# Moving the evacuation of the turned attention rows from VectorE to ScalarE, with the softmax reciprocals multiplied on GpSimd

## The chip, the core and the metric

The kernel runs on one core of a Trainium2 chip. Five engines work side by side, each through its own list of instructions in order: PE (TensorE, the matrix products), DVE (VectorE), ACT (ScalarE), POOL (GpSimd) and SP (SyncE, which here only issues DMA transfers). An instruction starts when its engine has come to it and the semaphores that it waits for have been raised. Products are written to PSUM, a small memory of eight banks that PE, DVE and ACT reach; POOL and the DMA transfers work on SBUF. The metric is the time of one execution in microseconds (us), the median of several runs.

## The reference, cut to what matters

Windowed attention with a distance bias, then a layer that sends each token to one of eight experts, then a dense two-layer network. The change lies in the first part and touches the rows that feed the second.

```python
scores = scale * np.matmul(q, k.transpose(0, 1, 3, 2))
scores = np.where(mask, scores + bias[None], -1000000000.0)      # mask: 0 <= i - j < 128
scores = scores - np.max(scores, axis=-1, keepdims=True)
attn = np.exp(scores)
attn = attn / (np.sum(attn, axis=-1, keepdims=True) + 1e-09)
attn_out = np.matmul(attn, v)                                    # 4 batches, 8 heads, 576 rows, 64 wide
x = attn_out.transpose(0, 2, 1, 3).reshape(B * S, H * D)         # 2304 rows of 512
...
logits = x @ w_gate + modality_bias[modality_id]
e_idx = np.argmax(logits, axis=1)
```

## The kernel before, in words

**Stages.** Attention fills the first 150 us. Then come the expert products, the chunks left over, and the dense network, which is by far the longest part; only attention is touched by the change. The program order of every engine is the order in which the code is written: nothing is reordered by a scheduler.

**Units.** Attention works on 40 units (b, t, hh): a batch b, a stretch t of 128 query rows (the fifth, t = 4, has 64), and a half hh of the eight heads. Two units make a row tile, and a group g of 128 output rows is one row tile, or the two short ones of two batches. There are 18 groups, of which 16 have t < 4. Line numbers are those of the kernel before, with L for line.

**A step.** The main loop takes step k and, in this order, issues: `smax` of unit k (DVE: pick the right columns, L289 or L284, then add the bias and take the row maximum, L294 or L296), the first half of `sexp` of unit k (ACT: the exponentials, L315 or L317), `sc` of unit k + 1 (PE: the scores into the banks called s and t), `tr` and `ev` of unit k - 2 (PE turns the exponentials, L337; ACT copies them out of the bank v, L344, L347 or L350; POOL masks the copy, L354 and L355), the second half of `sexp`, a first call of `background()`, `pv` of unit k - 3 (PE: the product with v, L374 or L381, into the bank W0, called x in the rows), and a second call of `background()`. For t = 4 two more ACT multiplications (L329) normalise the exponentials.

**The group's tail, `post`.** When both halves of a row tile are in W0, `post` is put on a list that `background()` works through, one piece at each call. Piece 1 (the second call in step k): ACT copies W0 to SBUF (L394). Piece 2 (the first call in step k + 1): PE multiplies that copy by `turned` (L403), which turns the rows back and also gives the gate's logits. The result has 4 blocks of 144 columns; three go to the bank called m, the fourth goes to the second half of W0, which is free at that time. DVE adds 1e-9 to the row sums and takes reciprocals (L405, L406). Piece 3 (the second call in step k + 1): DVE takes the result out of both banks and multiplies it by the reciprocals on the way (L418; for t = 4 it only copies, L416): 384 and 128 columns of rows (`row<-m`, `row<-x`) and 48 and 16 columns of logits (`ls<-m`, `ls<-x`). It then sums the logits (L419), and SP writes the rows to HBM (L420). The products `pv` of the next row tile's first half come between pieces 2 and 3 in the code, and write the first half of W0.

**Around it.** Every third group or so starts `route` (L450 to L508), a chain of small DVE operations with a few products, one piece at each call of `background()`. In the last third of attention the first expert slot is prepared between the units: gathers on POOL (L716), casts of weights and of gathered rows on ACT (L669, L730), the second half of a split on POOL (L672) or DVE (L734), and the first expert products on PE (L743).

Of the kernel before, what the change touches and what calls it, by code (L numbers as in the profile page):

```python
# [13 lines left out]
ALU = mybir.AluOpType  # L14
# [4 lines left out]
B, H, S, D = 4, 8, 576, 64  # L19
NTOK, DM = B * S, H * D  # L20
E, FF = 8, 1024
# [18 lines left out]
def row_of(g):  # L40
    return 128 * g + (SLOT if g >= CHECK else 0)
# [12 lines left out]
def attention_moe_kernel(ctx, tc, qh, kh, v, mid, wg, mb, w1, w2, win, wout, out):  # L54
    nc = tc.nc
    dve, act, pe, pool = nc.vector, nc.scalar, nc.tensor, nc.gpsimd
# [20 lines left out]
    def row(dt=F32):  # L77
        return take(("row", dt), 6, lambda: rowp.tile([128, DM], dt, tag="row", name="row"))

    def bank(tag, shape=(128, 512)):  # L80
        n = 1 if tag in "xm" else 2
        return take((tag, tuple(shape)), n, lambda: psum.tile(list(shape), F32, tag=tag, name=tag, bufs=n))
# [4 lines left out]
    xs = [[dram.tile([128, 2, 2, HT], F32, name=f"xs{j}_{i}") for i in range(7)] for j in range(NB)]  # L87
# [269 lines left out]
    def group(u):  # L357
        b, t, _ = u
        return 9 * (b // 2) + (8 if t == 4 else 4 * (b % 2) + t)
# [4 lines left out]
    def pv(u):  # L364
        b, t, hh = u
        o = st.pop(u)
        kb = [4] if t == 4 else [t - 1, t] if t else [t]
        for i in range(2):
            hp = 2 * hh + i
            if t < 4:  # L370
                for n, k_ in enumerate(kb):
                    for j in range(2):
                        h = 2 * hp + j
                        pe.matmul(W0[64 * j:64 * j + 64, hp, :], vS[b][:, k_, 64 * h:64 * h + 64], o[:, i, k_ - t + 1, j, :], start=n == 0, stop=n == len(kb) - 1, skip_group_check=True)  # L374
            else:
                c = slice(64 * (b % 2), 64 * (b % 2) + 64)
                for n in range(2):
                    r = 64 if n else 128
                    for j in range(2):
                        h = 2 * hp + j  # L380
                        pe.matmul(W0[64 * j:64 * j + 64, hp, c], vS[b][:r, 3 + n, 64 * h:64 * h + 64], o[:r, i, n, 0, 64 * j:64 * j + 64], start=n == 0, stop=n == 1, skip_group_check=True)  # L381
        if hh:
            todo.append(post(u))
# [3 lines left out]
    def post(u):  # L387
        b, t, _ = u
        g = group(u)
        if t < 4 or b % 2 == 0:  # L390
            xus[g] = row().rearrange("p (a b) -> p a b", a=4)
        xu = xus[g]
        c = slice(64 * (b % 2), 64 * (b % 2) + 64) if t == 4 else slice(0, 128)
        act.copy(xu[:, :, c], W0[:, :, c])  # L394
        if t == 4 and b % 2 == 0:
            return
        del xus[g]
        yield

        C = 128 + 2 * E  # L400
        xp = bank("m")[:, :3 * C].rearrange("p (a c) -> p a c", a=3), W0[:, 2:4, :].rearrange("p a b -> p (a b)")[:, None, :C]
        for i in range(4):
            pe.matmul(xp[i // 3][:, i % 3, :], xu[:, i, :], turned[:, i, :], start=True, stop=True)  # L403
        if t < 4:
            dve.tensor_scalar(rinv[b, t], rinv[b, t], 1e-9, None, op0=ALU.add)  # L405
            dve.reciprocal(rinv[b, t], rinv[b, t])  # L406
        yield
        xs = row()
        ls = sm.tile([128, H, E], F32, tag="ls", name="ls", bufs=2)
        r = rinv.pop((b, t)) if t < 4 else None  # L410
        for p, h0, n in ((xp[0], 0, 6), (xp[1], 6, 2)):
            hs = slice(h0, h0 + n)
            for o, w, d in ((xs.rearrange("p (h d) -> p h d", h=H)[:, hs, :], p[:, :, :128], D), (ls[:, hs, :], p[:, :, 128:], E)):
                o, w = o.rearrange("p (a j) d -> p a j d", j=2), w.rearrange("p a (j d) -> p a j d", j=2)
                if t == 4:
                    dve.tensor_copy(o, w)  # L416
                else:
                    dve.tensor_tensor(o, w, r[:, hs].rearrange("p (a j) -> p a j", j=2)[:, :, :, None].to_broadcast([128, n // 2, 2, d]), op=ALU.mult)  # L418
        dve.tensor_reduce(l_all[:, g, :], ls.rearrange("p h e -> p e h"), axis=AX.X, op=ALU.add)  # L419
        nc.sync.dma_start(out=xd[row_of(g):row_of(g) + 128, :], in_=xs)  # L420
        if g in gends:
            ready.append(route(g + 1 - gends[g], gends[g]))
# [362 lines left out]
    def expert_src(e, j):  # L785
        src = w1 if j < 4 else w2
        return src[bass.ds(e, 1), j % 4].rearrange("o p f -> (o p) f")
# [183 lines left out]
    n = len(units)  # L971
# [129 lines left out]
    for s in range(NSLOT):  # L1101
        n, nn = ({NSLOT - 1: SHORT, NSLOT - 2: MIDDLE}.get(i, SLOT) for i in (s, s + 1))
# [26 lines left out]
        if s == 2:  # L1129
            p = bank("v", (128, E))  # L1130
# [6 lines left out]
        for i in range((n + 127) // 128):  # L1137
# [3 lines left out]
            c = slice(128 * i, min(n, 128 * i + 128))  # L1141
# [24 lines left out]
    p = ps = None  # L1166
    held.append({})

    def chunk(src):
        r, h, l = (take(("w", dt), n, lambda: wpools["right"].tile([128, 1024], dt, tag="w", name="w")) for dt, n in ((F32, 2), (F32R, 4), (F32R, 4)))  # L1170
        nc.sync.dma_start(out=r, in_=src)
        act.copy(h, r)
        dve.tensor_tensor(l, r, h.bitcast(F32), op=ALU.subtract)
        return h, l

    le, lo = (loop_int[:, i].rearrange("p a b -> p (a b)") for i in range(2))
    with tc.For_i(4 * (NSLOT - 1), total, 1) as ci:
        e = nc.sync.value_load(le[0:1, bass.ds(ci, 1)], min_val=0, max_val=E - 1)
        o = pool.value_load(lo[0:1, bass.ds(ci, 1)], min_val=0, max_val=E * NCH - 1)
# [4 lines left out]
        for g in range(2):  # L1184
            r, p = row(), bank("v", (128, 4, 128))
# [12 lines left out]
        for f in range(8):  # L1198
            if f % 2 == 0:
                w = chunk(expert_src(e, 4 + f // 2))  # L1200
# [13 lines left out]
    ps, c = bank("t"), slice(128 * i, 128 * i + 128)  # L1214
# [203 lines left out]
    for n, (k, h) in enumerate(((0, 0), (0, 1), (1, 1), (1, 0))):  # L1418
        for c in range(2):
            p = bank("xmssvvxm"[2 * n + c])[:, :HT]  # L1420
# [102 lines left out]
```

## Time and profile before

| what | value |
|---|---|
| median of 3 runs | 758.87 us (757.5 to 758.89) |
| the profiled execution, its own time | 757.94 us |
| span of that execution, first to last instruction | 756.1 us |
| PE busy | 725.4 us (96%) |
| DVE busy | 499.8 us (66%) |
| ACT busy | 344.4 us (46%) |
| POOL busy | 302.9 us (40%) |

The profiled execution lies inside the range of the runs. The shares are averages over the whole program. What the change is worth is decided in the first 150 us, so the rows further down come from that stretch.

### The profile page before, as it was taken

What the parts mean: (1) busy time and instruction counts of PE and PEld (TensorE: products, weight loads), DVE (VectorE), ACT (ScalarE), POOL (GpSimd) and SP (SyncE); (2) the same over time, 40 slices, a digit from 0 to 9 for tenths busy, and PEclk for the clock granted to TensorE, in tenths of its full rate; (3) what the DMA queues carried; (4) which work ended last, traced back from release to release, by engine and by line L of the source; (5) the groups of instructions that cost most, each with busy time, mean ns of one, the idle gap of its engine ahead of it and who ended that gap; (6) DMA issues with size and microseconds to landing.
All of it is one profiled execution on the core that took longest, in us unless ns stands there. A gap on an engine that the chain in (4) does not pass through costs nothing.

```text
span 756.1 us, 13418 instructions
## 1 busy us (share of the span) xinstructions
PE 725.4 (96%) x4567; PEld 627.3 (83%) x4567; DVE 499.8 (66%) x1288; ACT 344.4 (46%) x839; POOL 302.9 (40%) x328
## 2 busy tenths in 40 slices
PE   7899889999999999998989999999999999999997
PEld 6777757777788889887878898989989889899896
DVE  7788877779976967776464664466754768442542
ACT  6676658424534545454555565423324234231230
POOL 4322345303454434536162464425534246240431
PEclk9999999999999999999999999999999999999999
DMA  8558450139488685960679671879719796295832
GB/s 268 187 178 279 136 199 32 58 126 360 153 323 273 231 288 181 380 236 16 236 251 367 258 320 57 341 291 394 280 72 360 281 410 242 83 360 202 329 112 84
DMA packets 71110, 174.57 MB, mean 231 GB/s; under 512 B 10032, under 2 KB 18480, under 8 KB 71040
## 3 DMA queue, kind: packets, MB, share of 16 engines
q1 hardware_dynamic: 68048, 163.93, 59.7%
q0 software_dynamic: 2992, 9.77, 3.3%
q8 instruction: 37, 0.61, 0.3%
q14 instruction: 33, 0.27, 0.1%
HBM read 117.76 MB, written 55.90 MB: 230 GB/s over the span
## 4 chain that ended last, share of the span: by engine, by line
PE 48%; DMA 3%; DVE 1%; ACT 0%; issue 0%; ACTq 0%; SPq 0%
PE v L743 17%; PE s L743 12%; PE t L743 12%; PE x L743 3%; PE m L743 3%; DMA w<-yd 2%; DMA yd<-row,idx 1%; DVE cr L1314 1%; DVE cr L1339 0%; DVE xq L1258 0%; PE s L1355 0%; ACT hd L1306 0%; PE s L1423 0%; DVE row L1375 0%; ACT xq L1254 0%
## 5 line engine op out<-in xcount | busy, mean ns | idle before, releaser
L1307 POOL TENSOR_TENSOR hd<-cr,hd 128x384 fp32r<-128x384 f32 x96 | 113.1, 1213 | 140.9 <-ACT hd L1306 140.9
L743 PE MATMUL v<-w,hd 128*128 128x512 f32 x576 | 137.1, 390 | 0.4 <-ACT w L1358 0.4
L743 PEld LDWEIGHTS v<-w,hd 128*128 128x128 f32 x576 | 107.8, 188 | 22.6 <-ACT w L1358 0.7
L743 PE MATMUL s<-xq,w 128*128 128x384 f32 x576 | 108.1, 335 | 0.7 <-DVE cr L1339 0.7
L743 PEld LDWEIGHTS s<-xq,w 128*128 128x128 f32 x576 | 100.9, 188 | 2.1 <-issue 1.0
L743 PE MATMUL t<-w,h 128*128 128x512 f32 (+1 forms) x408 | 98.8, 395 | 2.1 <-DVE w L1213 2.1
L694 POOL TENSOR_TENSOR row<-row 128x512 int32<-128x512 int32 x32 | 45.5, 1421 | 129.7 <-DVE row L693 86.3
L743 PEld LDWEIGHTS t<-w,h 128*128 128x128 f32 (+1 forms) x408 | 73.4, 183 | 19.7 <-issue 2.6
L1306 ACT CAST hd<-cr 128x384 fp32r<-128x384 f32 x96 | 49.3, 514 | 66.4 <-DVE cr L1314 63.4
L743 PE MATMUL t<-w,hd 128*128 128x512 f32 x288 | 69.2, 389 | 0.0
L743 PE MATMUL s<-w 128*128 128x512 f32 (+2 forms) x292 | 66.2, 378 | 1.1 <-DVE h L768 1.1
L1375 DVE SCALAR_TENSOR_TENSOR row<-v,gate,row 128x512 f32<-128x512 f32 x36 | 27.0, 750 | 56.6 <-PE v L743 54.4
L315 ACT ACTIVATE e<-x,m 128x128 f32<-128x128 f32 x128 | 50.4, 398 | 30.0 <-DVE m L294 30.0
L743 PEld LDWEIGHTS t<-w,hd 128*128 128x128 f32 x288 | 54.1, 188 | 11.2
L672 DVE TENSOR_TENSOR w<-w 128x1024 fp32r<-128x1024 f32 x37 | 51.1, 1387 | 17.6 <-ACT w L669 15.5
L743 PEld LDWEIGHTS s<-w 128*128 128x128 f32 x292 | 53.2, 188 | 9.5 <-DVE h L768 2.0
L1336 ACT COPY cr<-s 128x384 f32<-128x384 f32 x48 | 23.0, 481 | 73.7 <-PE s L743 73.5
L1314 DVE SCALAR_TENSOR_TENSOR cr<-cr 128x384 f32<-128x384 f32 x72 | 52.5, 729 | 2.5
L354 POOL TENSOR_SCALAR_AFFINE_SELECT pt<-pt 128x512 f32<-128x512 f32 (+1 forms) x32 | 18.7, 586 | 75.0 <-ACT pt L350 58.7
L669 ACT CAST w<-w 128x1024 fp32r<-128x1024 f32 (+1 forms) x43 | 41.9, 990 | 2.0 <-DMA w<-w 2.0
L1339 DVE TENSOR_TENSOR cr<-t,cr 128x384 f32<-128x384 f32 x24 | 13.3, 554 | 44.1 <-PE t L743 44.1
L686 ACT ACTIVATE row<-w 128x512 f32<-128x512 f32 x32 | 21.3, 672 | 29.2 <-POOL row L694 25.6
(323 smaller groups left out, 1434.7 us busy)
## 6 DMA issues: line engine op xcount, KB each, us to landing
xq<-xs SPq DMA_DIRECT2D x42, 768.0 KB
w<-w SPq DMA_DIRECT2D x40, 512.0 KB, 5.4
xs<-xq SPq DMA_DIRECT2D x21, 768.0 KB, 3.4
ya<-row SPq DMA_DIRECT2D x54, 256.0 KB, 2.1
row<-ya SPq DMA_DIRECT2D x54, 256.0 KB, 8.8
w<-win SPq DMA_DIRECT2D x16, 512.0 KB, 7.2
wc<-row SPq DMA_DIRECT2D x32, 256.0 KB, 3.4
w<-wout SPq DMA_DIRECT2D x16, 512.0 KB, 5.2
```

The source lines that it names most:

```text
L315: act.activation(e[:, i, j, :], x[:, i, j, :], AF.Exp, bias=m[:, i, j:j + 1], scale=-1.0, accum_out=rinv[b, t][:, h:h + 1])
L354: pool.affine_select(out=diag, in_=prev[:diag.shape[0]], pattern=[[0, 2], [0, 2], [1, n]], channel_multiplier=-1, compare_op=ALU.is_ge, **kw)
L669: act.copy(h[:, c], r[:, c])
L672: (eng or dve).tensor_tensor(l[:, c], r[:, c], h[:, c].bitcast(F32), op=ALU.subtract)
L686: act.mul(f, hi.bitcast(F32), 2.0 ** -112)
L694: pool.tensor_tensor(a, a, r, op=ALU.add)
L743: pe.matmul(ps, l, r, start=first and i == 0, stop=last and i == n - 1, **kw)
L1306: act.copy(gh, c)
L1307: pool.tensor_tensor(gl, c, gh.bitcast(F32), op=ALU.subtract)
L1314: dve.scalar_tensor_tensor(c, c, 0.0, c, op0=ALU.max, op1=ALU.mult)
L1336: act.copy(c, ps[q])
L1375: dve.scalar_tensor_tensor(o, ps, gate, o, op0=ALU.mult, op1=ALU.add)
```

## The change

The multiplication by the reciprocals is taken off the way out of PSUM for the rows. ACT copies the 384 and 128 columns of rows out of the two banks as they are (the new L413). DVE still takes the 48 and 16 columns of logits, multiplied. For t < 4, POOL then multiplies the whole row tile, 128 x 512 in SBUF, by the reciprocals in place (the new L421), and the write to HBM follows that.

```diff
         for p, h0, n in ((xp[0], 0, 6), (xp[1], 6, 2)):
             hs = slice(h0, h0 + n)
-            for o, w, d in ((xs.rearrange("p (h d) -> p h d", h=H)[:, hs, :], p[:, :, :128], D), (ls[:, hs, :], p[:, :, 128:], E)):
-                o, w = o.rearrange("p (a j) d -> p a j d", j=2), w.rearrange("p a (j d) -> p a j d", j=2)
-                if t == 4:
-                    dve.tensor_copy(o, w)
-                else:
-                    dve.tensor_tensor(o, w, r[:, hs].rearrange("p (a j) -> p a j", j=2)[:, :, :, None].to_broadcast([128, n // 2, 2, d]), op=ALU.mult)
+            act.copy(xs.rearrange("p (a c) -> p a c", a=4)[:, h0 // 2:(h0 + n) // 2, :], p[:, :, :128])
+            o, w = ls[:, hs, :].rearrange("p (a j) d -> p a j d", j=2), p[:, :, 128:].rearrange("p a (j d) -> p a j d", j=2)
+            if t == 4:
+                dve.tensor_copy(o, w)
+            else:
+                dve.tensor_tensor(o, w, r[:, hs].rearrange("p (a j) -> p a j", j=2)[:, :, :, None].to_broadcast([128, n // 2, 2, E]), op=ALU.mult)
+        if t < 4:
+            o = xs.rearrange("p (h d) -> p h d", h=H)
+            pool.tensor_tensor(o, o, r[:, :, None].to_broadcast([128, H, D]), op=ALU.mult)
         dve.tensor_reduce(l_all[:, g, :], ls.rearrange("p h e -> p e h"), axis=AX.X, op=ALU.add)
         nc.sync.dma_start(out=xd[row_of(g):row_of(g) + 128, :], in_=xs)
```

In the lists of the engines, PE and SP keep their order. On DVE the second group's tail reads as follows; `m` and `x` are the two banks, `ri` the reciprocals, and the bracket at a row's end names the engines whose semaphores it waits for (Activation is ACT).

```order
 L405 TENSOR_SCALAR ri<-ri 128x8
 L406 RECIPROCAL ri<-ri 128x8 [waits DVE_49]
-L418 TENSOR_TENSOR row<-m,ri 128x384 [waits DVE_49,PE_49]
-L418 TENSOR_TENSOR ls<-m,ri 128x48
-L418 TENSOR_TENSOR row<-x,ri 128x128 [waits PE_49,Activation_49]
-L418 TENSOR_TENSOR ls<-x,ri 128x16
-L419 TENSOR_REDUCE l_all<-ls 128x8 [waits DVE_49]
+L418 TENSOR_TENSOR ls<-m,ri 128x48 [waits DVE_49,Activation_49]
+L418 TENSOR_TENSOR ls<-x,ri 128x16 [waits Activation_49]
+L422 TENSOR_REDUCE l_all<-ls 128x8 [waits DVE_49]
```

The two multiplications of rows are gone, and each of the two that are left now carries a wait for ACT where it stood behind a wait for PE.

On ACT the copies come after the second half of the exponentials. Towards the end of attention other work stands ahead of them as well; this is the piece of the changed kernel's list around group 14's evacuation, with casts of weights (L672 in its numbering) and of gathered rows (L733).

```order
L315 ACTIVATE e,ri<-x,m 128x128 [waits DVE_49] x2
L672 CAST w<-w 128x512 [waits DMAHW1_49]
L672 CAST w<-w 128x512
L733 CAST w<-v 128x2x128 [waits PE_49]
L733 CAST w<-v 128x2x128
L413 COPY row<-m 128x384 [waits DMAHW5_49]
L413 COPY row<-x 128x128
L317 ACTIVATE e,rt<-x,m 128x128 [waits DVE_49,Activation_49]
```

The two rows of L413 are new there; in the kernel before, L317 followed the casts.

On POOL one multiplication per group stands behind the masks of the step. This is a piece of the changed kernel's list, in the middle of attention.

```order
L355 AFFINE_SELECT pt<-pt 128x2x256 [waits Pool_49]
L421 TENSOR_TENSOR row<-row,ri 128x512 [waits DVE_49,Activation_49]
L354 AFFINE_SELECT pt<-pt 128x2x256 [waits Activation_49]
L355 AFFINE_SELECT pt<-pt 128x2x256 [waits Pool_49]
L354 AFFINE_SELECT pt<-pt 128x2x256 [waits Activation_49]
```

Sixteen such rows of L421 are new on POOL, and nothing is taken from it.

## Rows read from the trace of the kernel before

**Rows 1.** Attention, 16 to 150 us: busy PE, PEld, DVE, ACT, POOL; clock, DMA.

```profile
16.00:150.00 134.00, 119.48 (x1462) 95.18 (x1455) 106.00 (x582) 88.10 (x342) 50.03 (x77) 0.99 0.47 157
```

**Rows 2.** Waits of PE, 15 to 155 us (us in total, times, longest).

```profile
PE m L403 <- ACT row L394: 3.9, 8, 0.9
...
PE v L469 <- ACT pt L350: 1.2, 1, 1.2
...
PE v L469 <- DVE t_acc L508: 1.1, 1, 1.1
```

**Rows 3.** Waits of ACT, 15 to 155 us.

```profile
ACT e L315 <- DVE m L294: 26.0, 14, 3.8
```

**Rows 4.** Waits of DVE, 15 to 155 us.

```profile
DVE row L418 <- PE x L374: 5.3, 9, 0.7
...
DVE row L418 <- PE x L381: 2.1, 3, 0.7
```

**Rows 5.** The page's costliest groups: an ACT copy of 384 columns out of PSUM.

```profile
L1336 ACT COPY cr<-s 128x384 f32<-128x384 f32 x48 | 23.0, 481 | 73.7 <-PE s L743 73.5
```

**Rows 6.** ACT's groups by shape, 0 to 160 us: a copy of 256 columns.

```profile
L347 ACT COPY pt<-v 128x256 f32<-128x256 f32 x8 | 2.9, 360 | 2.5 <-PE v L504 2.5
```

**Rows 7.** Timeline of DVE and ACT about group 10's evacuation (start, duration, idle before).

```profile
90.13 0.56 DVE L418 TENSOR_TENSOR row<-m,ri 128x384 f32<-128x384 f32 x1 [0.42 <-PE m L403]
...
90.58 0.40 ACT L315 ACTIVATE e<-x,m 128x128 f32<-128x128 f32 x1
90.60 0.20 DVE L418 TENSOR_TENSOR ls<-m,ri 128x48 f32<-128x48 f32 x1
91.48 0.29 DVE L418 TENSOR_TENSOR row<-x,ri 128x128 f32<-128x128 f32 x1 [0.68 <-PE x L374]
91.69 0.17 DVE L418 TENSOR_TENSOR ls<-x,ri 128x16 f32<-128x16 f32 x1
91.88 0.27 DVE L419 TENSOR_REDUCE l_all<-ls 128x8 f32<-128x64 f32 x1
...
92.78 0.40 ACT L317 ACTIVATE e<-x,m 128x128 f32<-128x128 f32 x1 [1.71 <-DVE m L296]
```

**Rows 8.** Timeline of ACT and DVE about group 8's evacuation.

```profile
77.20 0.39 ACT L315 ACTIVATE e<-x,m 128x128 f32<-128x128 f32 x1
77.75 0.27 DVE L419 TENSOR_REDUCE l_all<-ls 128x8 f32<-128x64 f32 x1
```

**Rows 9.** Timeline of ACT and DVE about group 14's evacuation.

```profile
129.17 0.65 ACT L730 CAST w<-v 128x256 fp32r<-128x256 f32 x2
129.53 0.28 DVE L419 TENSOR_REDUCE l_all<-ls 128x8 f32<-128x64 f32 x1
...
130.43 0.40 ACT L317 ACTIVATE e<-x,m 128x128 f32<-128x128 f32 x1 [0.61 <-DVE m L296]
```

**Rows 10.** Timeline of DVE, ACT and PE about group 15's evacuation.

```profile
136.35 0.27 DVE L419 TENSOR_REDUCE l_all<-ls 128x8 f32<-128x64 f32 x1
136.45 0.65 ACT L730 CAST w<-v 128x256 fp32r<-128x256 f32 x2 [1.11 <-PE v L724]
...
139.53 1.00 PE L403 MATMUL m<-turned,row 128*128 128x144 f32 x6 [0.75 <-ACT row L394]
```

**Rows 11.** Timeline of PE, ACT and DVE about group 9's evacuation.

```profile
83.11 1.09 PE L374 MATMUL x<-pt,vS 128*64 128x128 f32 x16
83.16 0.39 ACT L315 ACTIVATE e<-x,m 128x128 f32<-128x128 f32 x1
...
85.20 0.27 DVE L419 TENSOR_REDUCE l_all<-ls 128x8 f32<-128x64 f32 x1
```

**Rows 12.** Timeline of DVE and POOL: three comparisons with and without POOL's multiplications beside them.

```profile
138.38 2.78 DVE L493 TENSOR_SCALAR row<-iota,row 128x128 fp32r<-128x128 f32 x3
138.55 2.53 POOL L672 TENSOR_TENSOR w<-w 128x512 fp32r<-128x512 f32 x2 [0.21 <-ACT w L669]
...
153.39 0.85 DVE L493 TENSOR_SCALAR row<-iota,row 128x128 fp32r<-128x128 f32 x3
```

## The prediction

> **What bounds the kernel now.** The change touches attention only, so I read that stretch and not the whole span. Over its 134 us the four busy times are 119 us for PE, 106 for DVE, 88 for ACT and 50 for POOL [rows 1]. PE is the fullest, and it has 14.5 us in which it does nothing. Only those can be won, and any new wait of PE adds to them. So the next view is what PE waits for. The waits that bear on the change are for ACT's copy L394 of the attention product (3.9 us), for ACT's copy L350 (1.2), and for DVE's small sum L508 (1.1) [rows 2]. ACT itself waits 26.0 us for DVE's row maxima, in 14 waits [rows 3]. So ACT is late because DVE is late, and PE because ACT is late. The order in a group's tail makes the loop: PE's L403, then DVE's evacuation L418 and the sum L419, then the row maxima of the next unit, then ACT's exponentials, then L394, then PE's next L403.
>
> One more view shows what holds DVE inside the evacuation. Before its second half, the 128 columns in the bank W0, it waits for PE's products L374 or L381 in 9 + 3 = 12 of the 18 groups [rows 4], although these write other columns of that bank. In group 10 it could have gone on at about 90.8 and starts at 91.48, when PE has left the bank [rows 7].
>
> **What is removed.** DVE no longer moves the 384 and 128 columns. An instruction's worth on DVE is the distance to the next start: 90.13 to 90.60 is 0.47 us, and 91.48 to 91.69 is 0.21 [rows 7]. The first of these lies in front of the wait for PE in the 12 groups that have one, so there the gain is 0.21, and it is 0.68 in the other six.
>
> **What takes its place.** The two small multiplications that stay on DVE now wait for ACT's two copies. So DVE's restart, by which I mean the start of the sum L419 after which the next row maxima follow, no longer depends on DVE's own arrival but on when ACT comes to its copies, and ACT comes to them after its four exponentials of the step and whatever else is listed ahead. I price this as follows.
>
> - ACT's copy of 384 columns takes 0.48 us [rows 5]; two casts of 256 columns take 0.65 together where a copy of that size takes 0.36, so that the next instruction starts 0.07 before the end [rows 6, 9]. That gives 0.41 from start to start.
> - No row has 128 columns. The bounds are nothing and the 0.36 of 256 columns [rows 6]. By the 0.12 us that 128 columns make between 256 and 384 [rows 5, 6] it is 0.24, an estimate that I take.
> - From DVE's second small multiplication to the sum it is 0.19 [rows 7]. The handover from ACT to DVE is not in the rows shown; nothing and 0.10 bound it, and I take 0.04.
>
> So the restart comes at the later of (ACT free + 0.41) and (PE out of W0), plus 0.24 + 0.04 + 0.19 = 0.47.
>
> **Group by group.** In group 10 ACT's last exponential starts at 90.58 and takes 0.40, so ACT is free at 90.98 and through the first copy at 91.39. PE is out of W0 at 91.48, which decides. The restart is 91.95 against 91.88 [rows 7], 0.07 later. Ten of the twelve groups that wait for PE look like this one: nothing is gained there, although DVE does less. About seven of them have a wait of PE behind them: +0.5 in all.
>
> In group 8 ACT is free at 77.59, and the restart goes from 77.75 to 78.47 [rows 8]: +0.7, and PE's wait for L508 [rows 2], which follows the row maxima, takes all of it. Group 4 is the same with +0.5.
>
> In group 14 two casts of weights and two of gathered rows stand ahead of the copies. ACT is free of them at 129.17 + 0.58 = 129.75, the restart is 130.63 against 129.53, and ACT's L317, which had waited only 0.61 us for DVE [rows 9], slips by that 1.1. PE's wait of 1.2 us for L350 [rows 2] is the one that follows: +1.1.
>
> In group 15 the copies stand behind a cast that waits for PE until 136.45. The restart goes from 136.35 to 137.91 [rows 10], and ACT itself is delayed by its own two copies, 0.65. What arrives at PE's wait for L394 at 139.53 lies between that 0.65 and the 1.56 of the restart; I take the middle, +1.1.
>
> In group 9 it is the other way. ACT was idle from 83.55 and PE out of W0 at 84.2, long before DVE arrived, so the copies are done early: restart at 84.3 + 0.47 = 84.8 instead of 85.20 [rows 11], or -0.4. Groups 6, 16 and 17 are of this kind and read in the same way: -0.3, -0.4 and -0.5.
>
> The sum is 0.5 + 0.7 + 0.5 + 1.1 + 1.1 - 0.4 - 0.3 - 0.4 - 0.5 = **+2.3 us**.
>
> **What is hidden.** POOL gets 16 multiplications of 128 x 512. Two such take 2.53 us [rows 12], so one takes 1.27, and POOL has 84 us free in the stretch [rows 1]. In group 10 it could start at 91.72; the next mask needs ACT's copy, which follows the exponential that begins at 92.78 [rows 7] and so ends after 93.5. That cover is the wait of ACT for DVE; without it each multiplication would delay a mask by up to 1.27. The write of the rows to HBM goes out about 1.3 us later. Behind it in SP's list stand loads for row tiles far ahead, and the gathers of these rows follow groups later; if a load of weights at the end were short of time it would cost that 1.3 once.
>
> **A rule beside it.** DVE's wait for PE in group 10 is for the bank, not for the columns [rows 7]. The Trainium skill, in "PSUM — Partial Sum Buffer", section "PSUM bank collisions raise a hardware error", says that no two of PE, ACT and DVE may access one bank in the same partitions at a time, reads by ACT and DVE included, and that the compiler orders such accesses one behind the other. By that rule an evacuation split between ACT and DVE is done in turns, and the sum is the one above; without it the two would read side by side and the time would be that of the first rival. The trace agrees where PE and DVE meet, with the 0.68 us of group 10; no group of before has ACT and DVE meet in this way.
>
> **Rivals.**
>
> *DVE's relief decides (faster).* Place: the restart. Price: 12 x 0.21 + 6 x 0.68 = 6.6 us less of DVE [rows 4, 7]. By the same share of about two thirds of the groups that have a wait of PE behind them some 4 us reach PE: 754 us. It decides where ACT is free 0.41 us before PE leaves the bank and before DVE arrives. For it: group 9 [rows 11], and the 26 us in which ACT is idle [rows 3]. Against it: groups 8, 14 and 15, where DVE is ahead of ACT [rows 8 to 10]. Chance 0.20.
>
> *The delays are absorbed (no change).* ACT's added work is 18 x 0.65 = 11.7 us and fits into its 26 us of waiting [rows 3]. If the late copies of groups 8, 14 and 15 fall into slack of PE that I took for none, gains and losses cancel: 757.9 to 759 us. Chance 0.18.
>
> *POOL holds up DVE (much slower).* DVE's three comparisons take 2.78 us beside two multiplications of POOL and 0.85 alone [rows 12], so one POOL multiplication can cost DVE about 1 us. If DVE has such an operation within 1.27 us of the restart in five of the sixteen groups, that is 5 us on top of the 2.3: 765 us. Against it: what follows the restart in most groups are column picks and row maxima that read PSUM. Chance 0.12.
>
> **How the numbers follow.** My forecast has 0.50. Against the profiled execution's own 757.94 us it gives 760.2. The median of the runs is 0.9 above that execution, well inside their range; with the whole of it the forecast would be 761.2, and I take 760.7, in the middle. Its own range is 759 to 763. What a measurement of this kernel can tell from no change is about 0.2%, or 1.5 us. The range for 8 in 10 goes from 755.5, which takes in half of the first rival, to 766, which takes in the third. Of the forecast's 0.50 some 0.07 lies within 1.5 us, so with the second rival 0.25 is no change; faster is 0.21, with a little of the second rival's lower edge; slower is 0.54.
>
> **What would show it.** Right: DVE's L418 waits for ACT's L413 in most groups, PE's waits for L394 and L350 grow in groups 8, 14 and 15, and ACT's wait for DVE's maxima shrinks by about the 11.7 us of copies and no more. DVE's busy time falls by some 15 us and PE's waiting does not fall. Wrong: DVE waits for PE as before and the restart comes earlier; or DVE operations near L421 grow longer. The prediction would also fail if the burst of transfers near the first gathers, which POOL now issues around a multiplication, shifted against PE's work by some microseconds.

## The result, and the profile of the changed kernel

The changed kernel takes 763.05 us in the median of 10 executions (759.79 to 766.74), the kernel before 758.79 (756.90 to 760.09): a ratio of 1.0059, 95% interval 1.0037 to 1.0082. That is slower by 4.3 us where the forecast of 760.7 stood for some 2. It lies inside the range for 8 in 10 and 0.05 us beyond the forecast's own range, 759 to 763. The profiled execution took 764.12 us, with a span of 762.5.

The busy times of attention in the changed kernel, in the columns of [rows 1]; the stretch ends 6 us later because attention does:

```profile
16.00:156.00 140.00, 120.46 (x1460) 96.67 (x1451) 95.59 (x545) 98.42 (x378) 66.54 (x93) 0.98 0.46 150
```

DVE has lost 10 us, ACT has gained 10 and POOL 16, as the change says. PE does the same work and stands still for 140.00 - 120.46 = 19.5 us instead of 14.5. What PE, DVE and ACT wait for, from 15 to 160 us (the engine, what waits, what it waits for; us in total, times, longest):

```profile
PE m L403 <- ACT row L394: 5.7, 8, 1.1
PE v L472 <- ACT pt L350: 2.3, 1, 2.3
PE v L472 <- DVE t_acc L511: 1.8, 1, 1.8
...
PE s L274 <- issue: 1.4, 1, 1.4
PE x L374 <- DVE ls L418: 1.4, 1, 1.4
...
DVE ls L418 <- ACT row L413: 29.9, 23, 3.5
...
ACT e L315 <- DVE m L294: 18.5, 15, 3.1
```

Line numbers behind L418 are 3 higher than before. The three waits of PE that were to grow have grown: for L394 from 3.9 to 5.7, for L350 from 1.2 to 2.3, for the small sum from 1.1 to 1.8 [rows 2]. Two are new: 1.4 before the scores L274, and 1.4 of L374 for DVE's logits. DVE's waits are now for ACT's copies, and ACT waits 18.5 us for DVE's maxima where it waited 26.0 [rows 3].

In twelve groups of the kernel before, PE held up DVE inside the evacuation; they are called held groups here. One of them, group 10, in the timeline of the changed kernel (start, duration, engine, instruction, idle before); it answers to [rows 7]:

```profile
94.67 1.09 PE L374 MATMUL x<-pt,vS 128*64 128x128 f32 x16
94.98 0.39 ACT L315 ACTIVATE e<-x,m 128x128 f32<-128x128 f32 x1
...
95.37 0.46 ACT L413 COPY row<-m 128x384 f32<-128x384 f32 x1
95.81 0.27 ACT L413 COPY row<-x 128x128 f32<-128x128 f32 x1
95.86 0.21 DVE L418 TENSOR_TENSOR ls<-m,ri 128x48 f32<-128x48 f32 x1 [1.72 <-ACT row L413]
96.11 0.17 DVE L418 TENSOR_TENSOR ls<-x,ri 128x16 f32<-128x16 f32 x1
96.32 0.27 DVE L422 TENSOR_REDUCE l_all<-ls 128x8 f32<-128x64 f32 x1
```

ACT is free at 95.37 and takes 0.44 from start to start; PE leaves W0 at 95.76, so ACT decides by 0.05. DVE follows ACT's first copy by 0.03. The price list stands nearly as it was written: 0.46 and 0.27 us for the copies where 0.48 and 0.24 were taken, 0.44 from start to start where 0.41 was, and 0.03 for the handover where 0.04 was.

Group 14, where the casts lie ahead, answers to [rows 9]:

```profile
133.13 0.65 ACT L733 CAST w<-v 128x256 fp32r<-128x256 f32 x2
...
133.66 0.50 ACT L413 COPY row<-m 128x384 f32<-128x384 f32 x1
134.03 0.30 ACT L413 COPY row<-x 128x128 f32<-128x128 f32 x1
...
134.57 0.27 DVE L422 TENSOR_REDUCE l_all<-ls 128x8 f32<-128x64 f32 x1
...
135.87 0.56 ACT L350 COPY pt<-v 128x512 f32<-128x512 f32 x1
136.49 0.28 PE L472 MATMUL v<-row,upper 128*128 128x24 f32 x1 [2.30 <-ACT pt L350]
```

The sum began 0.4 us after the two casts began before, and begins 1.44 after them now. The 1.08 in between is found again, whole, in PE's wait for L350.

Two things that no term of the sum held are in the trace as well. The first is DVE beside POOL. These are rows of the changed kernel about groups 0, 11, 15 and 16:

```profile
21.13 1.04 POOL L421 TENSOR_TENSOR row<-row,ri 128x512 f32<-128x512 f32 x1 [0.92 <-ACT row L413]
...
21.48 0.73 DVE L230 CAST midf<-mids 128x18 f32<-128x18 int32 x1
...
24.58 0.89 PE L274 MATMUL s<-kS,qS 128*128 128x192 f32 x4 [1.41 <-issue]
...
103.59 1.04 POOL L421 TENSOR_TENSOR row<-row,ri 128x512 f32<-128x512 f32 x1 [1.43 <-ACT row L413]
...
104.11 0.54 DVE L536 TENSOR_SCALAR firsth<-r,r 1x8 f32<-1x8 f32 x1
...
142.76 1.04 POOL L421 TENSOR_TENSOR row<-row,ri 128x512 f32<-128x512 f32 x1 [1.94 <-ACT row L413]
...
143.11 0.72 DVE L323 TENSOR_SCALAR rt<-rt 128x2 f32<-128x2 f32 x1
...
148.35 1.04 POOL L421 TENSOR_TENSOR row<-row,ri 128x512 f32<-128x512 f32 x1 [0.40 <-ACT row L413]
...
148.96 0.48 DVE L453 TENSOR_TENSOR l_all<-l_all,lbias 128x24 f32<-128x24 f32 x1
```

A cast of 18 columns takes 0.73 us, an operation on eight numbers 0.54, one of two columns 0.72 and one of 24 columns 0.48, and all four end within 0.05 us of the end of POOL's multiplication (21.13 + 1.04 = 22.17, 103.59 + 1.04 = 104.63, 142.76 + 1.04 = 143.80 and 148.35 + 1.04 = 149.39).

The second is TensorE's clock. The windows of one us about PE's wait for L511 in the changed kernel (span, PE, PEld, DVE, ACT and POOL busy, granted clock, DMA share, GB/s):

```profile
81.00:82.00 1.00, 0.19 (x2) 0.00 (x0) 1.00 (x4) 0.00 (x0) 0.00 (x0) 1.00 0.43 156
82.00:83.00 1.00, 0.00 (x0) 0.00 (x0) 0.96 (x9) 0.81 (x5) 0.00 (x0) 1.00 0.53 167
83.00:84.00 1.00, 0.98 (x14) 0.79 (x18) 0.52 (x3) 1.00 (x5) 0.39 (x1) 1.00 1.10 327
84.00:85.00 1.00, 1.00 (x26) 0.83 (x27) 1.00 (x7) 1.00 (x4) 0.88 (x2) 0.94 1.06 395
85.00:86.00 1.00, 1.00 (x6) 1.00 (x5) 0.93 (x8) 0.77 (x5) 0.00 (x0) 0.50 0.06 21
```

PE stands still for 1.83 us and works again from 83.0; at 84.9 the granted clock falls from 1.00 (2.4 GHz) to 0.50 (1.2 GHz) and stays there until 88.3. A second such fall stands at 26.9 to 30.3, behind the new wait of 1.41 and one of 0.90. The profiled execution of the kernel before has one, from 111.8 to 115.3, behind a pause of 1.10.

### The profile page after: what moved, and what is told of

Same layout as the page of the kernel before. It is cut to its first block, busy times and chain, and to the rows that moved or that the text cites. A ratio compares the mean times of both kernels' runs of the same rounds, so it can differ in the third digit from the quotient of the medians.

```text
span 762.5 us, 13437 instructions
## 1 busy us (share of the span) xinstructions
PE 728.4 (96%) x4567; PEld 630.7 (83%) x4567; DVE 489.3 (64%) x1252; ACT 355.3 (47%) x875; POOL 318.6 (42%) x344
## 4 chain that ended last, share of the span: by engine, by line
PE 49%; DMA 2%; DVE 1%; ACT 0%; issue 0%; POOLq 0%; SPq 0%; POOL 0%
PE v L746 17%; PE t L746 13%; PE s L746 12%; PE x L746 3%; PE m L746 3%; DMA w<-yd 1%; DVE cr L1317 1%; DMA yd<-row,idx 1%; DVE cr L1342 0%; DVE xq L1261 0%; PE s L1358 0%; ACT hd L1309 0%; DVE row L1378 0%; ACT xq L1257 0%; DVE w L1222 0%
## 5 line engine op out<-in xcount | busy, mean ns | idle before, releaser
L746 PE MATMUL t<-w,h 128*128 128x512 f32 (+1 forms) x408 | 100.4, 399 | 2.1 <-DVE ids L1214 2.1
L315 ACT ACTIVATE e<-x,m 128x128 f32<-128x128 f32 x128 | 50.4, 396 | 22.5 <-DVE m L294 22.5
L672 ACT CAST w<-w 128x1024 fp32r<-128x1024 f32 (+1 forms) x43 | 41.9, 988 | 1.0 <-DMA w<-w 1.0
```

What stands on the lines that cost most here:

```text
L315: act.activation(e[:, i, j, :], x[:, i, j, :], AF.Exp, bias=m[:, i, j:j + 1], scale=-1.0, accum_out=rinv[b, t][:, h:h + 1])
L672: act.copy(h[:, c], r[:, c])
L746: pe.matmul(ps, l, r, start=first and i == 0, stop=last and i == n - 1, **kw)
```

## The experiments

Each execution comes with its mean granted clock. Over 201 executions of 16 kernel-and-set pairs (one execution of the kernel before, at 2506 us, is left out), with a level of its own for each pair, the time rises by 0.44 us (standard error 0.02) for every 0.001 of clock that is missing. The last column takes that out: the level at clock 1.000, less that of the kernel before in the same set. It is called the time at full clock below; it is worked out by this fit and not measured with the clock held, and the standard error of an entry is 0.3 to 0.5 us. The times compare within a set only: the kernel before is at 756.2, 759.1 and 756.0 us in the three sets. Expectations in whole times were made from its 758.8 and are to be read as differences to that.

| kernel | median us | before | ratio, 95% interval | mean clock (before) | at full clock, us |
|---|---|---|---|---|---|
| logits first | 756.10 | 756.19 | 0.9999 (0.9983 to 1.0014) | 0.9953 (0.9979) | -1.05 |
| no GpSimd | 760.55 | 756.19 | 1.0057 (1.0037 to 1.0078) | 0.9925 | +1.85 |
| four groups back | 757.00 | 756.19 | 1.0006 (0.9994 to 1.0019) | 0.9950 | -0.83 |
| bias later | 760.72 | 756.19 | 1.0053 (1.0034 to 1.0073) | 0.9925 | +1.64 |
| changed, again | 763.57 | 759.10 | 1.0064 (1.0048 to 1.0081) | 0.9923 (0.9939) | +3.93 |
| copy twice | 772.15 | 759.10 | 1.0159 (1.0125 to 1.0193) | 0.9882 | +10.07 |
| logits first, bias later | 756.63 | 759.10 | 0.9973 (0.9953 to 0.9993) | 0.9927 | -2.32 |
| pauses filled | 761.99 | 759.10 | 1.0043 (1.0026 to 1.0059) | 0.9958 | +3.90 |
| bias alone | 755.39 | 756.04 | 0.9995 (0.9986 to 1.0004) | 0.9974 (0.9982) | -1.10 |
| four groups only | 761.95 | 756.04 | 1.0088 (1.0069 to 1.0106) | 0.9952 | +4.80 |
| the combined, 15 back | 754.50 | 756.04 | 0.9982 (0.9968 to 0.9996) | 0.9951 | -2.65 |
| the combined, again | 755.49 | 756.04 | 0.9987 (0.9973 to 1.0001) | 0.9939 | -2.70 |

The second measure is read from the timelines: the time from a group's first product L403 to the start of its sum (L419 before), less the same time in the kernel before, in us. It is the restart by itself, free of what was late earlier. The forecast is the prediction's, with group 15's bound of 1.56. An f marks a group with a fall of the clock in it. Groups 1, 7, 11, 12 and 13 are left out; they are held groups, and in the changed kernel, again, they stand at +0.02 to +0.04.

```
group  forecast  changed,again  no GpSimd  four only  four back  copy twice  combined,again
0        +0.07       +0.03        +0.03      0.00      +0.03       +0.45        -0.20
2        +0.07       +0.06        +0.06      0.00      +0.06       +0.37        -0.23
3        +0.07       -0.17        -0.16      0.00      -0.16       +0.03        -0.40
4        +0.5        +0.49        +0.48     +0.47       0.00       +1.00        -0.21
5        +0.07       +0.02        +0.03      0.00      +0.02       +0.46        -0.21
6        -0.3        -0.29        -0.29     -0.14      -0.29       -0.01        -0.41
8        +0.7        +0.70        +0.71     +0.70      +0.04       +1.28        -0.61
9        -0.4        +0.03 f      -0.44     +0.03      -0.45       +0.74 f      -0.67
10       +0.07       +0.03        +0.03      0.00      +0.04       +0.47        -0.19
14       +1.1        +1.08        +1.07     +1.07       0.00       +1.59        -0.66
15       +1.56       +1.54        +2.31 f   +1.53       0.00       +3.27 f      +0.43
16       -0.4        -0.76        -0.76     -0.11      -0.63       -0.69        -0.15
17       -0.5        -0.66        -0.66      0.00      -0.66       -0.59        -0.65
```

**Logits first.** DVE reads its logits before ACT gets the banks.

```diff
-            act.copy(xs.rearrange("p (a c) -> p a c", a=4)[:, h0 // 2:(h0 + n) // 2, :], p[:, :, :128])
...
+        dve.tensor_reduce(l_all[:, g, :], ls.rearrange("p h e -> p e h"), axis=AX.X, op=ALU.add)
+        for p, h0, n in ((xp[0], 0, 6), (xp[1], 6, 2)):
+            act.copy(xs.rearrange("p (a c) -> p a c", a=4)[:, h0 // 2:(h0 + n) // 2, :], p[:, :, :128])
         if t < 4:
...
-        dve.tensor_reduce(l_all[:, g, :], ls.rearrange("p h e -> p e h"), axis=AX.X, op=ALU.add)
```

> DVE takes the logits of both banks and sums them before ACT is given the rows; everything else is as in the changed kernel. Theory (the loss is DVE's restart waiting behind ACT): the sum then starts 0.2 us after PE has left W0, which in the twelve groups held by PE is 0.21 us before the time of the kernel before, and in the others up to 0.68; DVE's waits for L413 (31 us) go, ACT waits for DVE instead, and of 6.6 us less of DVE about 4 reach PE: 753 to 757 us. Rival 1 (ACT's added 11.7 us of copies are what hurts, wherever DVE stands): 762 to 764 us, with PE's waits for L394 as large as now. Rival 2 (the multiplications on POOL hurt): also 762 to 764 us, since they stay.

The whole loss goes: ratio 0.9999, where the changed kernel has 1.0059. ACT makes the same copies and POOL the same multiplications, so it is the place of DVE behind ACT that made the loss. The gain of 4 us did not come: the kernel before is at 756.2 in this set, and what is gained is 1.05 us at full clock. Waits from 15 to 160 us in this kernel:

```profile
ACT row L420 <- DVE ls L417: 10.4, 14, 2.8
...
DVE ls L417 <- ACT row L420: 3.4, 3, 1.1
...
PE x L374 <- ACT row L420: 1.2, 1, 1.2
```

ACT now waits for DVE at the banks, 10.4 us in 14 waits, and still has 12.2 us of waits for DVE's maxima (L315). PE waits for a copy only twice, where ACT comes late: 1.2 us in group 15, and 0.9 of L381 in group 16.

**No GpSimd.** L421 is left out.

```diff
-        if t < 4:
-            o = xs.rearrange("p (h d) -> p h d", h=H)
-            pool.tensor_tensor(o, o, r[:, :, None].to_broadcast([128, H, D]), op=ALU.mult)
```

> The multiplication on GpSimd is left out, so the rows written are not divided by the softmax sums; the logits still are, so the routing is that of the reference. Theory (the copies on ACT make the loss, POOL costs about 0.6 us in the first group, where DVE's cast L230 takes 0.73 beside it): 761 to 763 us, DVE's waits for L413 still some 30 us. Rival (POOL holds up DVE or the masks): five or more operations of DVE get shorter by half a us and more, 756 to 759 us.

The ratio of 1.0057 is that of the changed kernel, so the loss in the median stays without POOL's multiplications. In this kernel L230, the L536 of the changed kernel, which is L533 here, and L323 take shorter times:

```profile
21.31 0.17 DVE L230 CAST midf<-mids 128x18 f32<-128x18 int32 x1
...
100.11 0.22 DVE L533 TENSOR_SCALAR firsth<-r,r 1x8 f32<-1x8 f32 x1
...
138.55 0.36 DVE L323 TENSOR_SCALAR rt<-rt 128x2 f32<-128x2 f32 x1
```

The 0.36 of L323 is still not its time alone, 0.15 to 0.17 us in other groups; it ends at 138.91, with a mask of POOL that ends at 138.88. The way from the sum to the next group's L403 is shorter than in the changed kernel by 0.57 us behind group 0, 0.32 behind group 11 and 0.37 behind group 15, 1.26 us in all, and elsewhere by no more than 0.03, falls of the clock and the stretch behind group 12 apart (there all kernels of one set differ alike from those of another, so it tells nothing). So POOL beside DVE is a part of the loss, 1.3 us by the timelines. At full clock the kernel is 2.1 us better than the changed one, across two sets (standard error 0.6). The median does not show it: the clock was low beside that of its set's kernel before, 0.9925 against 0.9979, with falls at 12 and at 131 us in its profiled execution, the latter behind PE's wait of 2.3 us for L350.

**Four groups back, and four groups only.** Groups 4, 8, 14 and 15 are put back to DVE; in the complement they alone are given to ACT and POOL.

```diff
         for p, h0, n in ((xp[0], 0, 6), (xp[1], 6, 2)):
             hs = slice(h0, h0 + n)
+            if g in (4, 8, 14, 15):
+                for o, w, d in ((xs.rearrange("p (h d) -> p h d", h=H)[:, hs, :], p[:, :, :128], D), (ls[:, hs, :], p[:, :, 128:], E)):
...
+                continue
             act.copy(xs.rearrange("p (a c) -> p a c", a=4)[:, h0 // 2:(h0 + n) // 2, :], p[:, :, :128])
...
-        if t < 4:
+        if t < 4 and g not in (4, 8, 14, 15):
```

What is left out is the loop of the kernel before; the complement has `not in` and `in` exchanged.

> Groups 4, 8, 14 and 15 are evacuated as before the change (DVE, with the multiplication), the other fourteen as after it. Theory (the restart behind ACT in these four groups is most of the loss: 0.5, 0.7, 1.1 and 1.5 to 1.8 us): 4 us less than the changed kernel, so 758 to 760 us, and the steps of about +0.5, +0.7, +1.1 and +1.5 at these groups go from the table of shifts, with the -0.3 to -0.7 of groups 6, 16 and 17 kept. Rival (the loss lies in the fourteen groups held by PE, in POOL or in the clock): 762 us or more.

> The complement of the kernel with four groups put back: only groups 4, 8, 14 and 15 are evacuated by ACT and POOL, the other fourteen as before the change. Theory (these four make the loss): the shifts of +0.5, +0.7, +1.1 and +1.5 to 1.8 stand in the table, nothing else does; 3.5 to 4 us slower at equal clock, ratio 1.004 to 1.007, slower than the changed kernel by the 1.5 us that groups 6, 9, 16 and 17 gained there less the 0.8 us of the first group. Rival (the loss needs all groups, through POOL or the clock): ratio below 1.002.

With the four back the ratio is 1.0006; with the four alone it is 1.0088. At full clock -0.83 and +4.80 add up to 3.97, and the changed kernel has +3.93. The table of restarts shows the four terms in the one and not in the other, within 0.04 us. The four-only kernel is 0.8 us slower than the upper end of what I expected, and the 3.77 us of its four terms don't hold that. In its timeline most of the rest has a place: the restart of group 13 is 0.41 later, because DVE comes to the bank m only 2.2 us behind L403 (1.0 in the kernel before), and the way to the next L403 is 0.28 longer behind group 15 and 0.22 behind group 5. PE's pauses in it:

```profile
81.19 0.28 PE L480 MATMUL v<-row,upper 128*128 128x16 f32 x1 [1.83 <-DVE t_acc L519]
...
132.10 0.28 PE L480 MATMUL v<-row,upper 128*128 128x24 f32 x1 [2.30 <-ACT pt L350]
...
138.65 1.09 PE L374 MATMUL x<-pt,vS 128*64 128x128 f32 x16 [1.37 <-DVE ls L426]
```

They are the long pauses of the changed kernel.

**Bias later, and bias alone.** The five operations L230 to L234 are issued one step later, in the changed kernel and in the kernel before.

```diff
-        for at, make in ((0, gate_weights), (1, tail_bias), (2, route_loads), (5, logit_bias), (15, dump_rows)):
+        for at, make in ((0, gate_weights), (1, tail_bias), (2, route_loads), (6, logit_bias), (15, dump_rows)):
```

> The five small operations of DVE that prepare the logits' bias (L230 to L234) are issued one step later, where POOL has no multiplication. Theory (POOL's first multiplication stretches L230 from 0.17 to 0.73 us, and this delays the second row tile's maxima, PE's L274 and, by the longer pause, the clock): the first 0.6 us of loss go, and if the fall of the clock at 27 us goes too, about 1.6 more: 761 to 762.4 us. Rival (neither matters, or the five operations cost as much a step later): 763 us, with the first loss of 2.4 us at group 2 still there.

> The kernel before with the five operations for the bias (L230 to L234) one step later, and nothing else: what of the gain of the combined kernel (ratio 0.9973) this shift alone makes. Theory (it takes 1.0 us off the second row tile's maxima, which had nothing to cover them, and the rest of the 2.3 us at equal clock is DVE's relief): 1.0 us faster at equal clock, ratio 0.998 to 0.9995. Rival (all of the gain is this shift): 2 us and more, ratio 0.997. Rival (given back later): 1.000.

In both the way from group 0's sum to the next L403 is 1.1 us shorter than in the kernel before, and at full clock the shift alone gives 1.10. In the changed kernel it takes away the 0.56 beside POOL too, and at full clock 2.3 in all. The median that I expected did not come: 1.0053 is not to be told from 1.0059. The mean clock of 0.9925 is as low as without the shift; the profiled execution has falls at 11.8 and, behind the wait of 1.83 for L511, at 80.

**Copy twice.** ACT makes its first copy two times.

```diff
-            act.copy(xs.rearrange("p (a c) -> p a c", a=4)[:, h0 // 2:(h0 + n) // 2, :], p[:, :, :128])
+            for _ in range(2 if h0 == 0 else 1):
+                act.copy(xs.rearrange("p (a c) -> p a c", a=4)[:, h0 // 2:(h0 + n) // 2, :], p[:, :, :128])
```

> ACT makes each copy of 384 columns twice, so that it is through 0.41 us later in every group. Theory (the restart is the later of ACT free + 0.41 and PE out of W0): with 0.82 in place of 0.41 ACT decides in the groups held by PE too, some 0.3 us late each, of which seven have a wait of PE behind them; groups 4, 8, 14 and 15 are another 0.4 later; the early groups do not move: 3 to 4.5 us slower than the changed kernel at equal clock. Rival (ACT has slack and these copies are not what holds DVE): no more than 1 us slower.

It is 6.1 us slower than the changed kernel at full clock, and 8.6 in the median: more than the theory gave. The tenth group of this kernel:

```profile
99.88 0.97 ACT L414 COPY row<-m 128x384 f32<-128x384 f32 x2
100.74 0.27 ACT L414 COPY row<-x 128x128 f32<-128x128 f32 x1
100.88 0.21 DVE L419 TENSOR_TENSOR ls<-m,ri 128x48 f32<-128x48 f32 x1 [2.20 <-ACT row L414]
```

The restart moves much as worked out, to +0.2 and up to +0.47 in the held groups that have no fall of the clock (group 3 to +0.03), and by another 0.5 to 0.6 in groups 4, 8 and 14. Group 6, which was not to move, moves by 0.28. What was wrong besides is that only seven of ten would pass it on. In the timelines the way from the sum to the next L403 differs from that of the kernel before by 0.17 us at most behind groups 1 to 7, 9 and 10: PE gets nearly the whole of it. The profiled execution has six falls of the clock, and the clock of the executions goes down to 0.980.

**Pauses filled.** PE repeats transposes in front of two pauses and one product in front of a third.

```diff
-            tr(units[k - 2])
+            tr(units[k - 2], 3 if k in (24, 38) else 1)
...
-            pv(units[k - 3])
+            pv(units[k - 3], 2 if k == 6 else 1)
```

> The changed kernel once more, unaltered, as the measure for the other three of this set. The set before gave each execution its mean granted clock, and over all of them the time rises by 0.48 us for each 0.001 of clock missing. Theory (the loss has two parts, the waits and falls of the clock that follow on longer pauses of PE): 0.5 to 0.7% slower than the kernel before again, mean clock 0.991 to 0.994 against 0.998, and 1.5 to 2.3 us slower at equal clock. Rival (the falls were chance): mean clock as in the kernel before, and the whole loss remains at equal clock.

> PE repeats products it has just made, with the same result, in front of three of its long pauses: eight transposes (1.2 us) ahead of the waits for L511 (1.83 us, group 8) and for L350 (2.3 us, group 14), and one attention product (1.1 us) ahead of the wait of 1.41 us at 24.6. No engine is held up by them by the rows of the trace; PE has 3.5 us more to do. Theory (falls of the clock follow on these pauses): mean clock 0.995 to 0.998 in place of 0.992, and 1.5 to 2.5 us faster than the changed kernel although PE does more. Rival (the falls are chance or come from elsewhere): clock 0.991 to 0.993, and the same time or up to 1 us more.

PE's two waits in this kernel:

```profile
79.22 1.53 PE L337 MATMUL v<-ident,e 128*128 128x128 f32 x12
81.71 0.28 PE L472 MATMUL v<-row,upper 128*128 128x16 f32 x1 [0.96 <-DVE t_acc L511]
...
130.69 1.47 PE L337 MATMUL v<-ident,e 128*128 128x128 f32 x12
133.60 0.28 PE L472 MATMUL v<-row,upper 128*128 128x24 f32 x1 [1.44 <-ACT pt L350]
```

The pauses shrink from 1.83 and 2.30 to 0.96 and 1.44, the mean clock rises from 0.9923 to 0.9958, and the kernel, though PE has more to do, is done 1.6 us earlier (standard error 0.5). At full clock the two kernels are equal, 3.90 and 3.93. So fewer falls come where the pauses are shorter: the clock is a second price of the same waits. The expectation for the changed kernel was met in its ratio and its clock, and missed in the rest: this set's kernel before has a low clock itself, 0.9939, so that only 0.7 of the 4.5 us are the clock's here, and 3.9 remain at full clock where I had put 1.5 to 2.3.

**Combined: logits first and bias later; then group 15 back.**

> The logits taken by DVE ahead of ACT's copies, and the five operations for the bias one step later. Theory (the first alone is worth 1.2 us against the kernel before at equal clock and loses 0.8 to 1.5 us in the first two groups, where POOL's multiplication lies beside L230; the second alone moved group 1 from +0.8 to -1.0): 2 to 3 us faster than the kernel before at equal clock, 0.2 to 0.4% in the ratio if the clock does not fall more often. Rival (what is gained in attention is given back in a wait behind it): ratio 0.999 to 1.001.

> The combined kernel once more, unaltered, as the measure for the one with group 15 put back: ratio 0.9953 to 0.9993 as in its first interval; rival (the first result was chance): 1.000.

> The combined kernel (logits first, bias later) with group 15 evacuated as before the change, since there ACT's copies stand behind a cast that waits for PE and PE then waits 1.16 us for the copy (L374 for ACT's L420). Theory: this wait goes and with it 0.4 to 0.9 us; ratio to the kernel before 0.995 to 0.997, clock as in the combined kernel. Rival (DVE's longer evacuation takes it all back): equal to the combined kernel.

The combined kernel is faster than the kernel before in the first set, 0.9973 (0.9953 to 0.9993), and 0.9987 in the second, whose interval ends at 1.0001; at full clock 2.3 and 2.7 us. Of these 1.1 are the bias. Putting group 15 back changes nothing that can be told (-2.65 against -2.70), as its rival said: the restart there comes 0.74 us later, and PE's wait of 1.16 us for ACT's copy becomes one of 1.0 for DVE.

In the timelines the relief is larger. From the first L403 on, the sum of group 17 comes 6.6 us earlier than in the kernel before, of which 2.3 lie behind group 12, where the sets differ; against the bias alone, in the same set, it comes 3.2 earlier. Yet the spans are 753.6 and 752.3. Here some of it is given back, in the combined kernel:

```profile
146.29 0.60 ACT L771 ACTIVATE h<-s 128x512 fp32r<-128x512 f32 x1 [0.58 <-PE s L747]
...
146.93 0.68 DVE L772 SCALAR_TENSOR_TENSOR h<-s,h 128x512 fp32r<-128x512 f32 x1
...
147.67 1.21 PE L747 MATMUL s<-w 128*128 128x512 f32 x4 [1.42 <-DVE h L772]
```

and the windows behind it:

```profile
148.00:149.00 1.00, 0.88 (x4) 0.38 (x2) 0.90 (x6) 0.74 (x1) 0.00 (x0) 1.00 0.88 225
149.00:150.00 1.00, 0.80 (x3) 0.83 (x4) 0.93 (x5) 0.30 (x1) 0.00 (x0) 0.58 0.58 238
150.00:151.00 1.00, 1.00 (x3) 0.75 (x3) 0.15 (x1) 0.00 (x0) 0.00 (x0) 0.50 0.09 37
...
155.00:156.00 1.00, 1.00 (x4) 0.71 (x3) 0.93 (x4) 0.00 (x0) 0.00 (x0) 0.51 0.90 266
```

PE arrives early at the first expert products, waits 1.42 us for a result that passes through ACT and DVE, and 1.5 us later the clock falls, for seven. With the bias alone this wait is 0.7 us and no fall follows. All four kernels with the logits first have the wait, 1.42 or 1.43 us, and a fall some 1.5 to 2 us behind it.

## Why the prediction was right, and where its size fell short

**What bounds the kernel: right.** The restart of DVE sets PE's time. Copy twice shows it for a loss: what the restart loses in a held group reaches the next L403 within 0.2 us. For a gain it is less regular. Of the 0.2 us that logits first takes off a held group's restart, in the combined kernel groups 2, 3, 7, 10 and 13 pass on the whole, groups 1 and 5 nothing, and the way behind group 11 is 0.83 longer.

**The restart as the later of (ACT free + 0.41) and (PE out of W0), plus 0.47: right.** In the table the forecast of groups 4, 8 and 14 is met within 0.02 us, and nine of the ten groups like group 10 are at +0.02 to +0.06 where 0.07 was said; group 3 is at -0.17. Group 15's bound of 1.56 is 1.54. In group 9 the working added the 0.47 to 84.3, though PE leaves W0 at 84.20 and ACT is free at 83.55 [rows 11]; by its own rule that is -0.5, and -0.44 came where no fall lay in the group.

**What reaches PE of it.** Here the working was too kind in one place and too hard in others. Of group 15's 1.56 I took 1.1; the whole reaches PE, and the way to the next L403 is another 0.27 longer. "About seven of ten have a wait of PE behind them" is wrong as a rule, but the term was small: the restarts of these ten groups add up to 0.1 us where 0.5 was taken. Groups 16 and 17 gave back 0.76 and 0.66 instead of 0.4 and 0.5. All 18 restarts add up to 1.8 us (changed, again, with group 9 at the -0.44 that it has without a fall), against a forecast of 2.3. This part of the sum was sound.

**"What is hidden": the step that failed in part.** POOL's multiplication was weighed against the masks that follow it, and that cover held. DVE was not given a price: the third rival had it, with five groups and 5 us, and I left it out of the sum. DVE is held in four groups, 0, 11, 15 and 16; behind the first three it costs 1.26 us by the timelines, up to 2.1 by the comparison at full clock. It is a term put at nothing, a third to a half of the 3.9 us at full clock, and not the whole of the loss: without POOL 1.85 us remain at full clock.

**The clock: no term at all.** The change made PE's pauses longer (1.13 to 1.83, 1.23 to 2.30, and new ones of 1.4), and falls of the clock follow on such pauses, though not on each. Between the mean clocks of 0.9923 and 0.9939 lie 0.7 us in the set with the changed kernel; between the 0.9925 of its close relatives and the 0.9979 of the kernel before in the first set lie 2.4. Filling the pauses gives 1.6 us back.

**The account.** Restarts 1.8, DVE beside POOL 1.3, clock 0.7: 3.8 us of the 4.5 in that set. Some 0.8 us at full clock stays open; with a standard error of 0.5 it may be chance. The timelines of attention do not hold it.

**Luck.** The direction and the place of the loss are the forecast's own. That 763.05 stayed inside the range is partly luck: its upper end, 766, was there for the third rival, and the clock, which no term held, could have cost more, as the 2.4 us show.

**The rivals.** DVE's relief deciding (754 us) was wrong for this order of reading, because DVE stands behind ACT; with the order turned, it is worth 1 to 1.6 us at full clock, far from 4. The delays were not absorbed: no slack was found. Of the signs that I named, two came out smaller. ACT's wait for DVE's maxima shrank by 7.5 us, not 11.7. DVE's busy time over the whole span fell from 499.8 to 489.3, not by 15: 18 pairs of row operations at 0.68 us from start to start are 12.2, and the four operations held beside POOL give 1.7 back.

**The rule beside it.** In groups 0 to 15 of the changed kernel DVE's read of the bank m follows the end of ACT's copy by 0.03 or 0.04 us, in groups 16 and 17, where DVE comes late, by 0.42 and 0.53; with logits first ACT's copy waits for DVE, 10.4 us in all. That agrees with what the Trainium skill says in "PSUM — Partial Sum Buffer", section "PSUM bank collisions raise a hardware error": the two don't read a bank side by side. Which one reads first is the difference between the ratios of 1.0059 and 0.9999.

## What to carry to other kernels

When one engine's evacuation is split between two that take turns at a bank, the engine whose next work is waited for reads first; with the copies behind it the time was that of the kernel before, and with the copies ahead of it 4 us were lost. Price a move by the waits it lengthens in the few places where the new engine comes late, not by the busy time it takes off: here the four groups where ACT comes late lost 3.8 us, and without them the loss was gone. Look at what the added engine holds up as well: POOL's multiplication cost DVE time in four places. And ask of each lengthened pause of PE whether the clock will hold across it.

## What the runs showed of the hardware that was not expected

**DVE behind POOL.** The cast L230 took 0.73 us in place of 0.17, the eight-number operation L536 0.54 in place of 0.22, the two-column L323 0.72 in place of 0.17 and the 24-column L453 0.48 in place of 0.18, each until POOL's multiplication of 1.04 us ended. Column picks (0.42 and 0.28 us) and maxima (0.28) beside other such multiplications kept their times. L453 is a tensor_tensor; the other three are a cast and two tensor_scalar operations. The Trainium skill, in "SBUF — State Buffer", section "Who interferes with whom", says that casts and tensor_scalar operations of DVE can take ports that GpSimd shares, and that the later of the two is then blocked for the other's whole instruction. The trace agrees in these three rows.

**The clock.** Falls from 2.4 to 1.2 GHz lasted 3 to 4 us, some twice as long and more. In the 14 profiled executions, up to 160 us, 18 of 22 falls came behind or at the end of a pause of PE of 1.3 to 2.8 us, the other four behind shorter ones of 0.5 to 1.1. They did not come behind each: 28 of the 46 such long pauses had none, the one of 2.30 before 136.5 in the changed kernel among them. So the same kernel has executions at 1.000 and at 0.988, and 7 us between them.
